# A decode kernel's last weights: the rest of w2 as 128 rows at the end, summed with wo's, and fewer waits on TensorE

## The chip, the cores and the metric

The kernel runs on one core of a Trainium2 chip. The metric is the device time of one execution in microseconds (us), the median of several runs. A profiled execution gives a trace with the instructions of each engine, the DMA packets and the landings of the transfers; a page sums it up. Its span begins with the first instruction and ends with the last one, and the execution's own time is a little longer.

Names used below: TensorE (PE; PEld is its loading of weights), VectorE (DVE), ScalarE (ACT), GpSimd (POOL), and SyncE (SP), which issues most transfers. A landing is the moment at which a transfer's semaphore has its full count of 16, one from each DMA engine.

## What is computed

One decode step of attention with 32 heads over a cache of 4096 keys, beside a dense layer of two matrices with a squared ReLU, mixed by a gate:

```python
g = sigmoid((x * gate_w).sum(-1))
q = x @ wq                                  # 512 -> 32 heads x 128
p = softmax(q . k_cache * 128**-0.5)        # 4096 keys a head
a = (p @ v_cache).reshape(4096) @ wo        # -> 512
r = max(x @ w1 + b1, 0)                     # 512 -> 1376
b = (r * r) @ w2 + b2                       # 1376 -> 512
out = g * a + (1 - g) * b
```

Everything is bfloat16 (both halves take the same x). The key and value caches are 32 MiB each, so nearly all of the kernel's traffic is theirs: 78.3 MB are read from HBM.

## The kernel before

**Tiles.** Four heads form a tile, so there are eight tiles (NT = 8). A tile of keys, and one of values, is 128 partitions by 128 rows of 128 numbers (32 KB a partition, 4 MB in all). A ring of five buffers of that size holds keys and values as they come. SyncE issues the loads in the order of the list LOADS (keys run two tiles ahead of values), each once its buffer is free (`free`, L300 to L308). The last entry but one in the list, "m", is the dense layer's: w1 (1376 KB, L336), the first 1280 rows of w2 with ten rows a partition (1280 KB, L337), and the last 96 rows of w2, one a partition on partitions 0 to 95 (96 KB, L338). After "m" come the values of the last tile, in four parts of 40, 36, 32 and 20 rows a partition (L331, by the table PARTS, L60), and after those the last 512 rows of wo as loads of 384 and 128 KB (L340). The other 3584 rows of wo are brought by GpSimd and SyncE earlier. The output goes out at L343.

**Keys.** The scores are split. VectorE multiplies and sums most rows (L716, 656 of them); the rest is transposed on TensorE (L509), copied out by ScalarE (L415) and multiplied with q (L524). The tile's maximum goes over VectorE and TensorE (`max_rows`, L531; `max_cols`, L536; L730, L733), ScalarE makes the exponentials (L434), and `pv` multiplies them with the values on TensorE (L555): one matmul for each row of the tile, 128 a tile. `den` (L564) sums the denominators, and `norm` (L746) divides and applies the gate.

**The end.** TensorE's order is written out by hand. After the last scores it does, in this order: `turn_a` and `spread_a` (L569, L576: the first 28 heads' results are turned), `out_a` (L585, 88 matmuls of wo into the accumulator `acc`), `max_cols`, `mlp_h` (L600, the first dense layer), `den` for the last tile, `mlp_out` (L612, 44 matmuls: the second dense layer, into its own accumulator `MO`), `pv` for the first part of the last values, `add_v` (L591, rows of wo that VectorE has summed meanwhile at L777 and L781), `pv` for the other three parts, and after `norm` `out_b` (L621, 16 matmuls of wo's rest into `acc`). Each part's `pv` waits for its own landing. VectorE adds `MO` to the scaled bias b2 (L817), later adds `acc` to that (L821), TensorE transposes the sum (L674), and VectorE copies it to where SyncE takes it (L823).

**The dense layer's rest.** 1376 = 10 x 128 + 96. The hidden layer is held as 128 partitions by 11 columns; the eleventh column has 96 rows. `b1c` holds b1 in that form, `mlp_bias` and `mlp` make max(h, 0)*h and multiply it by 1 - g (`omg`, L765).

**Waits.** Each instruction may be preceded by any number of waits on semaphores. In TensorE's part many are covered: by program order, or by another wait, they have always been met when they come. `pm` (L478) makes each use of one PSUM bank wait until the one before has been read.

Of the kernel before, what the change touches and what calls it, by code (L numbers as in the profile page):

```python
# [5 lines left out]
def bass_gated_mix__gqa_block_cached__dense_activation_squared_relu__decode_kernel(  # L6
# [25 lines left out]
    FG = 10  # L32
    FR = F - FG * 128
    SCALE = float(D) ** -0.5


    R = 4
# [21 lines left out]

    PARTS = {NT - 3: [0, 64, B], NT - 2: [0, 32, 64, 96, B], NT - 1: [0, 40, 76, 108, B]}  # L60

# [71 lines left out]
    with ctx:  # L133
# [19 lines left out]
        w2a = held("m")[:, W2:W3].rearrange("p (g n) -> p g n", g=FG)  # L153
        w2b = held("m")[0:FR, W3:W3 + DM]
        W4 = W3 + DM
# [46 lines left out]
        hp = sb("hp", [128, FG + 1], fp32)  # L202
        hs = sb("hs", [128, FG + 1], bf16)
        b2g = sb("b2g", [128, 4], fp32)
        fin = sb("fin", [128, 4], bf16)
# [17 lines left out]
        H = pX[:, 256:256 + FG + 1]  # L223
        MO = pX[:, 288:292]
        B1 = pM[:, 288:288 + FG + 1]
# [54 lines left out]
        s_h = sem("s_h")  # L280
        s_mo = sem("s_mo")
        s_fb = sem("s_fb")
        s_vs = sem("s_vs")
# [27 lines left out]
        def started(eng):  # L311
            eng.wait_ge(s_qps, NT)
            eng.wait_ge(s_g, 4)
            eng.wait_ge(s_b1c, 2)


        @block.sync
        def _(eng):
            for n, (kind, j) in enumerate(LOADS):
                free(eng, n)  # L320
                if n == SLOTS - 1:
                    started(eng)
                    for p, st, k, q in STRIPS[len(RUNS):]:
                        a, b = W[p:p + st * (k - 1) + 1:st, :], woa_v[q:q + k, :]
                        if k == 1:
                            a, b = [v.rearrange("p (a n) -> p a n", a=2) for v in (a, b)]
                        eng.dma_start(a, b).then_inc(s_wr, 16)
                if kind == "v" and j in PARTS:
                    for w in range(len(PARTS[j]) - 1):
                        part = slice(PARTS[j][w] * 128, PARTS[j][w + 1] * 128)  # L330
                        eng.dma_start(held("v", j)[:, part], v_v[j][:, part]).then_inc(s_vl[j, w], 16)  # L331
                elif kind in "kv":
                    eng.dma_start(held(kind, j), (k_v if kind == "k" else v_v)[j])\
                       .then_inc(s_l[n % SLOTS], 16)
                elif kind == "m":
                    eng.dma_start(held("m")[:, 0:W2], w1_v).then_inc(s_w[0], 16)  # L336
                    eng.dma_start(held("m")[:, W2:W3], w2_v).then_inc(s_w[1], 16)  # L337
                    eng.dma_start(w2b, B_w2[FG * 128:F, :]).then_inc(s_w[2], 16)  # L338
            for c in range(len(TS) - 1):
                eng.dma_start(wob_sb[:, TS[c]:TS[c + 1], :], wob_v[:, TS[c]:TS[c + 1], :])\  # L340
                   .then_inc(s_wo[c], 16)
            eng.wait_ge(s_f4, 1)
            eng.dma_start(out[0, 0, :].rearrange("(j p) -> j p", p=128), fin4).then_inc(s_out, 16)  # L343
# [110 lines left out]
        def _(eng):  # L454
# [11 lines left out]
            for n in range(FG + 1):  # L466
                M = 128 if n < FG else FR
                mm = eng.matmul(B1[0:M, n:n + 1], b1r[:, n:FG * 128:FG] if n < FG else b1r[:, FG * 128:F],
                                ident[0:1, 0:1], start=True, stop=True)
# [5 lines left out]

            read = [(s_b1c, 2)]

            def pm(sem, count):  # L478
                for w in read:
                    eng.wait_ge(*w)  # L480
                read[:] = [(sem, count)]
# [15 lines left out]
            def transposes(u):  # L497
# [3 lines left out]
                for k in range(2):  # L501
                    n = 2 * u + k
                    if n >= 3:
                        eng.wait_ge(s_ev, n - 2)
# [8 lines left out]
            def scores(u):  # L513
                j, w = u // U, u % U
                if w == 0:
                    if j >= 2:
                        eng.wait_ge(s_cp, R * (j - 1))
                    eng.wait_ge(s_qc, j + 1)
                for k in range(2):
# [8 lines left out]
            def max_rows(j):  # L528
                eng.wait_ge(s_mp, j + 1)
                pm(s_gm, j + 1)  # L530
                eng.transpose(MT[0:1, :], mp[:, j:j + 1], identf[:, :]).then_inc(s_mt, 1)  # L531

            def max_cols(j):
                eng.wait_ge(s_dg, j + 1)
                pm(s_nm, j + 1)
                eng.matmul(MB[:, j:j + 1], gx[0:1, j % 2, :], onesf[0:1, 0:1],  # L536
# [23 lines left out]
            def den(c):  # L560
                a, b = GR[c]
                eng.wait_ge(s_e, b)
                pm(s_rd, c + 1)
                eng.matmul(DEN[:, a:b], onesf[:, :], RS[:, a:b], start=True, stop=True).then_inc(s_den, 1)  # L564

            def turn_a():
                eng.wait_ge(s_on, NG - 1)
                eng.wait_ge(s_ev, 2 * NU)
                eng.transpose(KP[0][0:NA, 0:128], onorm[:, 0:NA], ident[:, :]).then_inc(s_at, 1)  # L569

            def spread_a():
                eng.wait_ge(s_ac, 1)
                eng.wait_ge(s_cp, R * NT)
                eng.wait_ge(s_sel, 1 + len(STRIPS))
                for c in range(4):
# [4 lines left out]
            def out_a():  # L580
                eng.wait_ge(s_ac, 2)
                eng.wait_ge(s_wk, 1)
                for t in range(TP):
# [10 lines left out]
            def mlp_h():  # L594
                eng.wait_ge(s_w[0], 16)
                for n in range(FG + 1):
                    M = 128 if n < FG else FR
                    for t in range(4):
                        lhs = w1_sb[:, t, n:FG * 128:FG] if n < FG else w1_sb[:, t, FG * 128:F]
                        mm = eng.matmul(H[0:M, n:n + 1], lhs, xcol[:, t:t + 1],  # L600
                                        start=(t == 0), stop=(t == 3))
                mm.then_inc(s_h, 1)

            def mlp_out():
                eng.wait_ge(s_w[1], 16)
                eng.wait_ge(s_w[2], 16)
                eng.wait_ge(s_hs, 1)
                for n in range(FG + 1):
                    M = 128 if n < FG else FR
                    w = w2a[:, n, :] if n < FG else w2b  # L610
                    for j in range(4):
                        mm = eng.matmul(MO[:, j:j + 1], w[:, j * 128:(j + 1) * 128], hs[0:M, n:n + 1],  # L612
                                        start=(n == 0 and j == 0), stop=(n == FG and j == 3),
                                        skip_group_check=True)
                mm.then_inc(s_mo, 1)

            def out_b(c):
                eng.wait_ge(s_wo[c], 16)
                for h in range(TS[c], TS[c + 1]):
                    for j in range(4):  # L620
                        mm = eng.matmul(acc[:, j:j + 1], wob_sb[:, h, j * 128:(j + 1) * 128],  # L621
                                        onorm[:, NA + h:NA + h + 1], start=False, stop=(h == NZ - 1),
                                        skip_group_check=True)
                if c == len(TS) - 2:
                    mm.then_inc(s_acc, 1)

# [37 lines left out]
            den(NG - 1)  # L664
            mlp_out()
            for u in range((NT - 1) * U, NU):
# [4 lines left out]
            for c in range(len(TS) - 1):  # L671
                out_b(c)
            eng.wait_ge(s_fin, 1)
            eng.transpose(KP[2][0:4, 0:128], fin[:, :], ident[:, :]).then_inc(s_fT, 1)  # L674
# [3 lines left out]
        def _(eng):  # L678
            eng.memset(zeros, 0.0).then_inc(s_dz, 1)
            eng.memset(b1c[:, :], 0.0).then_inc(s_dz, 1)  # L680
            eng.wait_ge(s_dz, 2)
            eng.wait_ge(s_x, 32)
            eng.tensor_tensor_reduce(grow, xrow, grow, 1.0, 0.0, ALU.mult,
# [15 lines left out]
            eng.wait_ge(s_b1, 1)  # L699
            eng.tensor_copy(b1c[:, 0:FG], B1[:, 0:FG]).then_inc(s_b1c, 1)  # L700
            eng.tensor_copy(b1c[0:FR, FG:FG + 1], B1[0:FR, FG:FG + 1]).then_inc(s_b1c, 1)

# [49 lines left out]
            def mlp_bias():  # L752
                eng.wait_ge(s_h, 1)
                eng.wait_ge(s_b1c, 2)
                for p, n in cells:
                    eng.tensor_tensor(hr[p, n], H[p, n], b1c[p, n], ALU.add).then_inc(s_hv, 1)

            def mlp():
                eng.wait_ge(s_hv, 1)
                for p, n in cells:  # L760
                    eng.scalar_tensor_tensor(out=hp[p, n], in0=hr[p, n], scalar=0.0, in1=hr[p, n],
                                             op0=ALU.max, op1=ALU.mult).then_inc(s_hv, 1)
                eng.wait_ge(s_hv, 2)
                for p, n in cells:
                    eng.tensor_scalar(hs[p, n], hp[p, n], omg[p, 0:1], None, ALU.mult).then_inc(s_hs, 1)  # L765

# [47 lines left out]
            recip(NG - 1)  # L814
            eng.wait_ge(s_mo, 1)
            eng.wait_ge(s_g, 4)
            eng.tensor_tensor(b2g[:, :], MO, b2g[:, :], ALU.add).then_inc(s_fb, 1)  # L817
            norm(NG - 1)
            eng.wait_ge(s_acc, 1)
            eng.wait_ge(s_fb, 1)  # L820
            eng.tensor_tensor(fin[:, :], acc[:, 0:4], b2g[:, :], ALU.add).then_inc(s_fin, 1)  # L821
# [33 lines left out]
```

## Time and profile before

| | us |
|---|---|
| median of three runs | 193.54 |
| lowest and highest | 193.41, 193.60 |
| the profiled execution | 193.49 |
| its span | 192.1 |

Of the span TensorE is busy for 57% (109.9 us), VectorE for 83%, ScalarE for 43%, GpSimd for 12%. The queue that SyncE feeds moves 75.37 MB in 4452 packets and takes 92.9% of the 16 DMA engines' time; GpSimd's queue moves 2.95 MB, and two queues bring instructions (16 packets with 0.26 MB, and 14 with 0.11 MB). The mean rate is 410 GB/s.

How to read it: in the timeline a line has the start, the time from the first start to the last end, the engine, the line of the kernel, the operation, what it writes and reads, how many there are, and in brackets how long the engine sat idle ahead of it and what ended that. "issue" there means that the engine waited for nothing that the profile shows. In the table by stretches each row has the stretch, its length, the busy time and count of each engine (PE, PEld, DVE, ACT, POOL), the clock granted to TensorE, the busy share of the DMA engines and the GB/s that they moved.

### The profile page before, as it was taken

Reading aid. Unit: us, or ns where it says so; the run is one execution under the profiler, and the core shown is the slowest. Engines: PE = TensorE matmul, PEld = TensorE weight load, DVE = VectorE, ACT = ScalarE, POOL = GpSimd, SP = SyncE. Lnnn points to the kernel's source line nnn. Section 1 sums busy time; section 2 is a strip of 40 time slices with the busy share of each in tenths; the row PEclk is TensorE's granted clock in tenths of the full one; section 3 lists DMA queues with packets and bytes.
Section 4 is the critical chain, followed back from the end, with each engine's and each line's share of the span. In section 5 each row is a group of like instructions: output and inputs, shape, how many; then the busy total and the mean of one; then the engine's idle time right before and its main releaser. Section 6 shows DMA issues by size and latency. Waiting matters only on the chain.

```text
span 192.1 us, 6035 instructions
## 1 busy us (share of the span) xinstructions
PE 109.9 (57%) x2056; PEld 97.1 (51%) x2058; DVE 158.8 (83%) x1387; ACT 82.7 (43%) x204; POOL 22.9 (12%) x56
## 2 busy tenths in 40 slices
PE   0139665544614653397469255935876488449884
PEld 0123344434513542297459145924876378448873
DVE  0310299999999999999999998998999799998721
ACT  2104776743833663078339232933744383001300
POOL 7760000995000000000000000000000000000000
PEclk9999999555555555555555555555855555555555
DMA  6999999999999999999999999999999999999991
GB/s 225 431 437 437 437 438 426 432 438 432 423 428 416 423 432 413 447 404 433 416 432 416 440 428 437 425 421 437 420 421 416 406 426 411 422 418 382 407 386 68
DMA packets 5456, 78.71 MB, mean 410 GB/s; under 512 B 1285, under 2 KB 1895, under 8 KB 2024
## 3 DMA queue, kind: packets, MB, share of 16 engines
q1 hardware_dynamic: 4452, 75.37, 92.9%
q0 software_dynamic: 960, 2.95, 3.8%
q8 instruction: 16, 0.26, 0.6%
q14 instruction: 14, 0.11, 0.1%
q10 hardware_dynamic: 14, 0.01, 0.0%
HBM read 78.32 MB, written 0.00 MB: 408 GB/s over the span
## 4 chain that ended last, share of the span: by engine, by line
DVE 48%; DMA 41%; SPq 6%; PE 3%; issue 1%; DVEq 0%
DVE ring L716 45%; DMA ring<-in_A_k_cache_dram 26%; DMA ring<-in_A_v_cache_dram 15%; SPq L331 5%; DVE S L716 2%; PE pO L555 1%; PE KP L509 1%; DVE gm L730 1%; DVE gx L733 0%; PE pQ L621 0%; PE pM L564 0%; PE pM L536 0%; SPq L337 0%; SPq L338 0%; SPq L294 0%
## 5 line engine op out<-in xcount | busy, mean ns | idle before, releaser
L716 DVE CUSTOM_DVE_ANT_0 ring<-ring,qb 128x128 bf16<-128x128 bf16 x656 | 140.6, 283 | 2.4 <-DMA ring<-in_A_k_cache_dram 2.4
L415 ACT ACTIVATE kT<-KP 128x768 bf16<-128x768 bf16 (+1 forms) x64 | 46.4, 783 | 48.7 <-PE KP L509 48.4
L509 PE MATMUL KP<-ident,ring 128*128 128x128 bf16 x368 | 43.0, 300 | 21.8 <-DMA ring<-in_A_k_cache_dram 18.6
L716 DVE DVE_READ_ACCUMULATOR2_ANT S<- 128x1 f32 x656 | 51.8, 79 | 0.1
L509 PEld LDWEIGHTS KP<-ident,ring 128*128 128x128 bf16 x368 | 35.6, 139 | 23.9 <-DMA ring<-in_A_k_cache_dram 19.0
L555 PE MATMUL pO<-E,ring 128*128 128x4 bf16 x640 | 19.8, 166 | 2.8 <-DMA ring<-in_A_v_cache_dram 2.2
L555 PEld LDWEIGHTS pO<-E,ring 128*128 128x128 bf16 x640 | 18.9, 105 | 3.4 <-DMA ring<-in_A_v_cache_dram 2.4
L434 ACT ACTIVATE E<-S,nM 32x128 bf16<-32x128 f32 x32 | 18.5, 579 | 0.9
L555 PE MATMUL pX<-E,ring 128*128 128x4 bf16 x384 | 11.9, 166 | 4.7 <-DMA ring<-in_A_v_cache_dram 4.7
L555 PEld LDWEIGHTS pX<-E,ring 128*128 128x128 bf16 x384 | 11.3, 103 | 5.2 <-DMA ring<-in_A_v_cache_dram 5.1
L426 ACT ACTIVATE nM<-pM 128x1 f32<-128x1 f32 x8 | 1.4, 170 | 23.0 <-PE pM L536 23.0
L531 PE MATMUL pM<-identf,mp 128*1 128x128 f32 x8 | 3.1, 384 | 13.9 <-DVE mp L723 13.9
L536 PE MATMUL pM<-onesf,gx 1*128 1x1 f32 x16 | 4.5, 345 | 9.1 <-DVE gx L733 9.1
L536 PEld LDWEIGHTS pM<-onesf,gx 1*128 1x128 f32 x16 | 3.8, 291 | 9.8 <-DVE gx L733 9.7
L524 PE MATMUL pQ<-qcol,kT 128*128 128x4 bf16 x176 | 7.8, 170 | 1.0 <-ACT kT L415 0.9
L531 PEld LDWEIGHTS pM<-identf,mp 128*1 128x1 f32 x8 | 0.7, 91 | 15.2 <-DVE mp L723 15.0
L524 PEld LDWEIGHTS pQ<-qcol,kT 128*128 128x128 bf16 x176 | 7.6, 111 | 1.3 <-ACT kT L415 1.3
L434 ACT ACTIVATION_READ_ACCUMULATOR E<-S,nM 32x1 f32 x32 | 8.1, 253 | 0.0
L386 POOL MEMSET tick<- 1x1 f32 x1 | 0.1, 90 | 66.9 <-DMA W<-in_A_wo_dram 66.9
L378 POOL DMA_DIRECT2D W<-in_A_wo_dram x14 | 8.0, 574 | 0.0
L524 PE MATMUL pS<-qcol,kT 128*128 128x4 bf16 x192 | 7.8, 168 | 0.0
L363 POOL TENSOR_SCALAR_AFFINE_SELECT selA<-selA 28x36 bf16<-28x36 bf16 (+6 forms) x22 | 7.4, 335 | 3.2 <-POOL selA L358 0.2
(83 smaller groups left out, 97.6 us busy)
## 6 DMA issues: line engine op xcount, KB each, us to landing
ring<-in_A_k_cache_dram SPq DMA_DIRECT2D x8, 4096.0 KB, 30.1
ring<-in_A_v_cache_dram SPq DMA_DIRECT2D x5, 4096.0 KB, 29.2
ring<-in_A_v_cache_dram SPq DMA_DIRECT2D x5, 1024.0 KB, 28.8
W<-in_A_wq_dram SPq DMA_DIRECT2D x1, 4096.0 KB, 12.6
ring<-in_A_v_cache_dram SPq DMA_DIRECT2D x2, 2048.0 KB, 27.5
W<-in_A_wo_dram POOLq DMA_DIRECT2D x2, 768.0 KB, 18.2
ring<-in_B_w_dram SPq DMA_DIRECT2D x1, 1376.0 KB, 25.0
ring<-in_B_w_dram SPq DMA_DIRECT2D x1, 1280.0 KB, 28.2
```

The source lines that it names most:

```text
L331: eng.dma_start(held("v", j)[:, part], v_v[j][:, part]).then_inc(s_vl[j, w], 16)
L363: eng.affine_select(out=part, in_=part, compare_op=ALU.not_equal, fill=1.0, base=-st * q, pattern=[[st, 4], [-1, st * (k - 1) + 1]], chann ...
L378: eng.dma_start(W[p:p + st * (k - 1) + 1:st, :], woa_v[q:q + k, :], max_dma_last_dim=16384).then_inc(s_wp[n], 16)
L415: eng.activation(kT[:, n % NC, 0:HB[u // U] * 128], KP[n % 3][:, 0:HB[u // U] * 128], ACT.Copy).then_inc(s_ev, 1)
L434: eng.activation(E[rows, j % NE, :, r], S[rows, j % NS, :], ACT.Exp, bias=nM[rows, j:j + 1], scale=SCALE, accum_out=RS[rows, R * j + r:R * ...
L509: mm = eng.transpose(KP[n % 3][:, y * 128:(y + 1) * 128], held("k", j)[:, b * 128:(b + 1) * 128], ident[:, :])
L524: mm = eng.matmul(S2[j % 2][:, c:c + R], kT[:, n % NC, y * 128:(y + 1) * 128], qcol[:, R * j:R * j + R], start=True, stop=True)
L531: eng.transpose(MT[0:1, :], mp[:, j:j + 1], identf[:, :]).then_inc(s_mt, 1)
L536: eng.matmul(MB[:, j:j + 1], gx[0:1, j % 2, :], onesf[0:1, 0:1], start=True, stop=True).then_inc(s_mb, 1)
L555: mm = eng.matmul(O(R * j, R * j + R), held("v", j)[:, b * 128:(b + 1) * 128], E[:, j % NE, b, :], start=(b == 0), stop=(b == B - 1), skip ...
L716: ins = eng.tensor_tensor_reduce(kb, kb, qb[:, j, :], 1.0, 0.0, ALU.mult, ALU.add, S[:, j % NS, b:b + 1])
L730: eng.tensor_reduce(g, MT[0:1, :].rearrange("a (r p) -> a r p", r=R), AX.X, ALU.max)\
```

## The change

- The load of w2's rest takes the last 128 rows of w2 (rows 1248 to 1375) instead of the last 96, on all 128 partitions, and is issued after wo's rest instead of ahead of the last values: 128 KB for 96 KB.
- The 32 rows that are thereby loaded twice count once: the hidden layer's eleventh column now has 128 rows too (the last 128 columns of w1, the last 128 numbers of b1), and a new tile `omw`, 1 - g everywhere and 0 in the first 32 rows of that column, replaces `omg` in the product (L765).
- The second dense layer is summed into `acc`, where wo's sums are, so `MO`, the semaphores s_mo and s_fb and VectorE's addition (L817) go. Its first ten columns (40 matmuls) stay where they were; the four matmuls of the eleventh come after `out_b`, and carry the semaphore that lets VectorE make `fin`.
- The last tile's values come in parts of 40, 40, 36 and 12 rows.
- On TensorE 31 covered waits are dropped: in `transposes`, `scores`, `max_rows`, `max_cols`, `den`, `turn_a`, and `spread_a` (which takes over the wait for wo's rows from `out_a`).

```diff
-    PARTS = {NT - 3: [0, 64, B], NT - 2: [0, 32, 64, 96, B], NT - 1: [0, 40, 76, 108, B]}
+    PARTS = {NT - 3: [0, 64, B], NT - 2: [0, 32, 64, 96, B], NT - 1: [0, 40, 80, 116, B]}
...
-        w2b = held("m")[0:FR, W3:W3 + DM]
+        w2b = held("m")[:, W3:W3 + DM]
...
-                    eng.dma_start(w2b, B_w2[FG * 128:F, :]).then_inc(s_w[2], 16)
             for c in range(len(TS) - 1):
                 eng.dma_start(wob_sb[:, TS[c]:TS[c + 1], :], wob_v[:, TS[c]:TS[c + 1], :])\
                    .then_inc(s_wo[c], 16)
+            eng.dma_start(w2b, B_w2[F - 128:F, :]).then_inc(s_w[2], 16)
...
-            def pm(sem, count):
+            def pm(sem, count, covered=()):
                 for w in read:
-                    eng.wait_ge(*w)
+                    if w[0] not in covered:
+                        eng.wait_ge(*w)
...
-                    if n >= 3:
+                    if k and n >= 3:
                         eng.wait_ge(s_ev, n - 2)
...
-                if w == 0:
-                    if j >= 2:
-                        eng.wait_ge(s_cp, R * (j - 1))
-                    eng.wait_ge(s_qc, j + 1)
+                if u == 0:
+                    eng.wait_ge(s_qc, 1)
...
-                pm(s_gm, j + 1)
+                pm(s_gm, j + 1, (s_qc, s_nm, s_rd))
...
-                pm(s_nm, j + 1)
+                pm(s_nm, j + 1, (s_gm,))
...
-                pm(s_rd, c + 1)
+                pm(s_rd, c + 1, (s_nm,) if c >= NG - 2 else ())
...
-                eng.wait_ge(s_ev, 2 * NU)
...
-                eng.wait_ge(s_cp, R * NT)
-                eng.wait_ge(s_sel, 1 + len(STRIPS))
+                eng.wait_ge(s_wk, 1)
...
-                        lhs = w1_sb[:, t, n:FG * 128:FG] if n < FG else w1_sb[:, t, FG * 128:F]
-                        mm = eng.matmul(H[0:M, n:n + 1], lhs, xcol[:, t:t + 1],
+                        lhs = w1_sb[:, t, n:FG * 128:FG] if n < FG else w1_sb[:, t, F - 128:F]
+                        mm = eng.matmul(H[:, n:n + 1], lhs, xcol[:, t:t + 1],
...
+            def mlp_out(n):
+                if n in (0, FG):
+                    eng.wait_ge(s_w[1 if n < FG else 2], 16)
+                if n == 0:
+                    eng.wait_ge(s_hs, 1)
+                w = w2a[:, n, :] if n < FG else w2b
+                for j in range(4):
+                    mm = eng.matmul(acc[:, j:j + 1], w[:, j * 128:(j + 1) * 128], hs[:, n:n + 1],
+                                    start=False, stop=(n == FG), skip_group_check=True)
+                if n == FG:
+                    mm.then_inc(s_acc, 1)
...
             den(NG - 1)
-            mlp_out()
+            for n in range(FG):
+                mlp_out(n)
...
             for c in range(len(TS) - 1):
                 out_b(c)
+            mlp_out(FG)
...
+            eng.memset(omw[:, :], 1.0).then_inc(s_dz, 1)
...
+            eng.memset(omw[0:FO, FG:FG + 1], 0.0).then_inc(s_dz, 1)
...
+            eng.tensor_copy(b1c[:, :], B1).then_inc(s_b1c, 1)
+            eng.wait_ge(s_dz, 3)
+            eng.tensor_scalar(omw[:, :], omw[:, :], omg[:, 0:1], None, ALU.mult).then_inc(s_g, 1)
...
-                    eng.tensor_scalar(hs[p, n], hp[p, n], omg[p, 0:1], None, ALU.mult).then_inc(s_hs, 1)
+                    eng.tensor_tensor(hs[p, n], hp[p, n], omw[p, n], ALU.mult).then_inc(s_hs, 1)
...
-            eng.wait_ge(s_mo, 1)
-            eng.wait_ge(s_g, 4)
-            eng.tensor_tensor(b2g[:, :], MO, b2g[:, :], ALU.add).then_inc(s_fb, 1)
             norm(NG - 1)
             eng.wait_ge(s_acc, 1)
-            eng.wait_ge(s_fb, 1)
+            eng.wait_ge(s_g, 4)
             eng.tensor_tensor(fin[:, :], acc[:, 0:4], b2g[:, :], ALU.add).then_inc(s_fin, 1)
```

## The prediction

> **What bounds the kernel now.** I read the 40 slices of the page first: from 5 us to 187 us the 16 DMA engines are busy, so the transfers set the pace, whatever the chain of waits says (it runs through VectorE because VectorE frees the buffers, but the queue always holds work).
>
> ```profile
> DMA  6999999999999999999999999999999999999991
> GB/s 225 431 437 437 437 438 426 432 438 432 423 428 416 423 432 413 447 404 433 416 432 416 440 428 437 425 421 437 420 421 416 406 426 411 422 418 382 407 386 68
> DVE 48%; DMA 41%; SPq 6%; PE 3%; issue 1%; DVEq 0%
> ```
>
> The rate is not even: slice 37 (173 to 178 us) falls to 382. The table by stretches shows where (last three columns: TensorE clock, DMA share, GB/s).
>
> ```profile
> 173.00:174.00 1.00, 0.71 (x9) 0.31 (x9) 0.55 (x4) 0.00 (x0) 0.00 (x0) 0.50 1.01 425
> 174.00:175.00 1.00, 1.00 (x40) 1.00 (x41) 0.93 (x4) 0.00 (x0) 0.00 (x0) 0.50 1.04 389
> 175.00:176.00 1.00, 1.00 (x44) 1.00 (x41) 0.96 (x2) 0.00 (x0) 0.00 (x0) 0.50 1.04 346
> 176.00:177.00 1.00, 1.00 (x20) 0.97 (x18) 0.96 (x2) 0.03 (x1) 0.00 (x0) 0.50 1.01 374
> 177.00:178.00 1.00, 1.00 (x20) 1.00 (x19) 0.93 (x3) 0.94 (x4) 0.00 (x0) 0.50 1.04 368
> 178.00:179.00 1.00, 1.00 (x21) 1.00 (x19) 0.75 (x1) 0.97 (x4) 0.00 (x0) 0.50 0.97 389
> 179.00:180.00 1.00, 0.68 (x11) 0.59 (x9) 0.25 (x2) 0.60 (x4) 0.00 (x0) 0.50 0.99 418
> ```
>
> The engines are full, but move less: against 420 the five stretches lack 31+74+46+52+31 = 234 KB, or 0.56 us. The trace's packet records say what runs there. The 1 KB packets of the 96-row load of w2 (L338) go through eight of the engines from 174.30 to 175.65 and through the other eight from 176.26 to 177.97; the 10,240-byte packets beside them, on all engines, take 450 to 550 ns instead of 385, from 174.8 to 176.1 and from 176.8 to 178.3: the same two intervals, 0.4 to 0.5 us later, about the time from a packet's end to its landing (wo's last packet ended at 189.31 and landed at 189.73). Other 1 KB packets do no such harm: the two loads of wo's rest (L340, 128 partitions) raise the 5,120-byte packets beside them from 196 to at most 205 ns. Nor is it the arithmetic: out_a and mlp_h (L585, L600) run on past the ends of the two intervals, and VectorE's L781 runs again from 180.27 at 412 to 436 GB/s.
>
> The end of the kernel, by the timeline:
>
> ```profile
> 186.66 1.25 PE L555 MATMUL pO<-E,ring 128*128 128x4 bf16 x35 [0.48 <-issue]
> ...
> 188.45 0.69 PE L555 MATMUL pO<-E,ring 128*128 128x4 bf16 x20 [0.54 <-DMA ring<-in_A_v_cache_dram]
> 189.25 0.22 DVE L746 SCALAR_TENSOR_TENSOR onorm<-pO,gcol,rden 128x4 bf16<-128x4 f32 x1 [5.73 <-PE pO L555]
> ...
> 189.54 0.57 PE L621 MATMUL pQ<-onorm,ring 128*128 128x1 bf16 x16 [0.40 <-DVE onorm L746]
> 190.15 0.16 DVE L821 TENSOR_TENSOR fin<-pQ,b2g 128x4 bf16<-128x4 f32 x1 [0.68 <-PE pQ L621]
> ```
>
> The last values land at 188.40; 20 matmuls, norm, 16 matmuls of wo, fin. Two clocks run here side by side: landing records of the slowest engine give w1 174.61, w2 178.21, its 96 rows 178.52, the four value parts 181.57, 184.35, 186.85, 188.40, wo's rest 189.41 and 189.73. The 13th wo matmul needs the last of these and starts at about 189.86 (189.54 plus 12 steps of 0.027), only 0.13 us later.
>
> **The change, part by part** (against the profiled run: span 192.1, time 193.49, so 1.39 lies around it; the median shown is 193.54, 0.05 above).
>
> *The load of w2's rest.* It leaves its place before the last values: -0.31 on everything behind (178.52 - 178.21). It comes back as 8 rows an engine at the end: wo's last 128 KB are the same shape, 189.73 - 189.41 = +0.32. What becomes of the slowing is not shown, so both ends: it goes wholly, or follows the load to the end. The slowest engine took 178.21 - 174.61 = 3.60 us for w2's 1280 KB and 181.57 - 178.52 = 3.05 for the first value part, also 1280 KB: 0.55 is the price, as the table gave. I take -0.54, because the nearest row for 1 KB packets on 128 partitions at the end (wo's rest) shows no slowing. Last landing: 189.73 - 0.31 - 0.54 + 0.32 = 189.20.
>
> The Trainium skill gives a reason: "DMA: Bandwidth & Descriptors", The descriptor swizzle, has each DMA engine of a 128-partition transfer write one SBUF port of its own, and its section on why a DMA increments its semaphore by 16 spreads 96 partitions over 16 engines too, six each, which then can't match the ports' eights. By that rule the slowing belongs to the 96 rows and the first rival below would have no chance; the trace agrees in time and place, but all engines slow alike, where a clash of ports would pick some, so that rival keeps the chance that the rows give it.
>
> SP: the four value parts are issued one issue (0.47 us) earlier, and w2's load after L340's second, which ends at 174.65. Even if that issue takes 7.6 us as its neighbour's did, it is out by 182.3, seven us ahead of its landing. SP's next task, the output, comes at 190.9.
>
> *Parts 40, 40, 36, 12.* No bytes change. Moved by -0.85 and the sizes (9,216 to 10,240 bytes a row: +0.27; 8,192 to 9,216: +0.28; both by the landings of the old parts; 5,120 to 3,072: -0.55, which closes the sum), the parts land at 180.72, 183.77, 186.55 and 187.55. Part 1 waits for mlp_out anyway (181.8), part 2 for add_v (185.16, which waits for VectorE's L781, untouched). Part 3 starts at 186.60, 36 steps of 0.027 end at 187.6; the last 12 start then, the last of them at 187.9. From there before's own distances: 0.28 to norm, 0.29 to wo: 188.47; the first wo load lands at 189.41 - 0.85 = 188.56, so 188.6. 16 matmuls: the last at 189.03, after the landing of wo's second load at 188.88. The 20-matmul step lost eight, 0.21 us, but this chain is no longer the later one.
>
> *Second layer summed into wo's accumulator.* Its last four matmuls move behind wo's and wait for the last landing, 189.20: start 189.25, the fourth at 189.35. Behind that wait on TensorE stand only the final transpose, and fin on VectorE. Before, the last wo matmul started at 189.95. So **-0.60**. VectorE loses L817 (0.13 us at 183.38, in a wait of 5.73: worth nothing). Without cover by the landing, the four extra matmuls would cost 0.11.
>
> *Start.* VectorE gets a memset and a 0.15 us multiply (as L694) and one copy of b1c instead of two (0.17 + 0.14): it waits from 14.0 to 17.4 for qcol. hs by a product of tensors: 0.17 (as L756) for 0.23, while TensorE waits; 0. The last column group of w1 and b1 as 128 columns: same count of matmuls; 0.
>
> *31 waits.* TensorE is idle 43% of the span and is ended by data; 0 directly. But they move something: code. The instruction queue fetched 16 blocks of 16 KB. In before, TensorE stops inside part 2 of the values, where nothing waits: 33 matmuls, 0.65 us, then three more at 186.66 (the "issue" line). The stop before that is den at 180.22, 0.5 after its input; between them lie 127 matmuls and 127 weight loads and a few waits, one block. The packet records have fetches at 177.61 and 184.30, each about 1.06 long. So a block comes 6.4 us after the block before it was entered. Today it hides: part 3 lands at 186.85. With 31 slots fewer (if each wait is one) and 8 moved behind, the stop moves 39 slots, to after the 13th matmul of part 3, which runs at 186.97. The block before is entered between 180.2, as now, and 180.6 (its own predecessor's start moves 15 matmuls, 0.4, back in out_a), so the code is there at 186.6 to 187.0. From that matmul to the last one of all it is 2.0 us (23 + 12 + 20 steps, norm and its gaps), and the last one waits for data until 189.35: code up to 187.3 costs nothing. I take 0.
>
> The Trainium skill's "Runtime: NRT & Kernel Launch", Instruction fetch mechanics, gives TensorE room for 2048 instructions and calls the fetch hidden; by it this cost would be nil at any place. By it the last two rivals below would have no chance; the trace disagrees (0.65 us in the middle of 36 matmuls).
>
> **Sum:** 193.49 - 0.60 = 192.89 for the profiled run; 192.94 by the median. Forecast 192.95.
>
> **The rivals.**
> - *The slowing follows the load,* or its cause is another and it stays. For: it came with these bytes of w2, and 128 rows are a third more. Against: wo's rest. Then the last landing is 189.73 - 0.31 + 0.32 = 189.74, up to +0.18 with a third more: 193.45 to 193.75, 0.22.
> - *TensorE takes over.* Code after 187.3, so that the last matmul starts 2.0 after it; at 187.6 that is 189.6: -0.35, 193.2. For: the stop above. Against: the slack. 193.1 to 193.4, 0.14; a slowing that goes only in part ends here too.
> - *Slower: the code comes much later.* Place: after the 13th matmul of part 3; price: each us late, one us, from 187.3 on; it decides at 187.95 (no gain left), and costs 0.4 at 188.35. For: after it no landing covers a stop. Against: that asks for 7.8 us from block to block where the trace has 6.4. 193.95 and above, 0.07.
>
> **How the numbers follow.** Forecast 0.57 (192.75 to 193.1). Range: from 0.2 below the forecast (slice rates alone vary by that) up to 193.6, most of the first rival; left out are the third, the rest of the first and a little below. 0.2% is 0.39 us, about what a measurement of this kernel can tell from no change. Faster by more means below 193.15: the forecast and a third of the second rival, 0.62. Within: 0.30. Slower: 0.08.
>
> **What would show it.** Right: 410 or more GB/s through w1, w2 and the first value part; part 1 landed near 180.7; the last four L612-like matmuls starting some 0.3 us after wo's, released by the load. Wrong: packets of 450 ns or more beside the 1 KB ones at the end (first rival), or an "issue" gap within the 36 matmuls of part 3 (the others). If the rate at 174 to 178 stays low with the load gone, its cause was another, and the time stays near 193.5.

## The result

| | before | after |
|---|---|---|
| median of six runs each, us | 193.56 (193.39 to 193.66) | 192.91 (192.84 to 193.23) |
| the profiled execution, us | 193.49 | 192.9 |
| its span, us | 192.1 | 191.5 |

The ratio after/before is 0.9973, with a 95% interval from 0.9962 to 0.9985: faster by about 0.5 us (0.3 to 0.7). The forecast was 192.95, within 192.75 to 193.6.

The page of the changed kernel, the same three lines as were shown of before (DMA share and GB/s in 40 slices, then the chain by engine):

```profile
DMA  6999999999999999999999999999999999999992
GB/s 226 432 438 438 438 440 428 438 411 450 411 443 411 421 412 421 438 429 431 414 447 421 428 426 428 431 417 424 428 419 424 411 428 409 421 415 428 417 382 70
DVE 48%; DMA 40%; SPq 7%; PE 3%; issue 1%; DVEq 0%
```

Slice 37 has gone from 382 to 428 GB/s. The others are what they were, to within the wobble of single slices (up to some 30 either way). In the stretches (columns as before, the last is GB/s):

```profile
174.00:175.00 1.00, 1.00 (x42) 1.00 (x41) 0.93 (x4) 0.00 (x0) 0.00 (x0) 0.50 1.05 440
175.00:176.00 1.00, 1.00 (x44) 1.00 (x41) 0.96 (x2) 0.00 (x0) 0.00 (x0) 0.50 1.05 440
176.00:177.00 1.00, 1.00 (x20) 0.97 (x18) 0.96 (x2) 0.06 (x1) 0.00 (x0) 0.50 0.95 399
177.00:178.00 1.00, 1.00 (x20) 1.00 (x20) 0.93 (x3) 0.94 (x4) 0.00 (x0) 0.50 1.11 457
178.00:179.00 1.00, 1.00 (x20) 1.00 (x20) 0.73 (x1) 0.95 (x4) 0.00 (x0) 0.50 0.90 369
```

Single rows swing (457 beside 369), because a packet's bytes are booked in one stretch. So the mean of the five is what counts: 421 GB/s, where before had 373. TensorE, VectorE and ScalarE do the same there as before, so the arithmetic is not what made the difference.

The end of the kernel, by the timeline:

```profile
186.71 1.44 PE L553 MATMUL pO<-E,ring 128*128 128x4 bf16 x48 [0.66 <-DMA ring<-in_A_v_cache_dram]
188.26 0.22 DVE L741 SCALAR_TENSOR_TENSOR onorm<-pO,gcol,rden 128x4 bf16<-128x4 f32 x1 [5.10 <-PE pO L553]
...
188.70 0.57 PE L614 MATMUL pQ<-onorm,ring 128*128 128x1 bf16 x16 [0.55 <-DMA ring<-in_A_wo_dram]
...
189.26 0.27 PE L605 MATMUL pQ<-hs,ring 128*128 128x1 bf16 x4
189.57 0.16 DVE L814 TENSOR_TENSOR fin<-pQ,b2g 128x4 bf16<-128x4 f32 x1 [1.09 <-PE pQ L605]
```

Parts 3 and 4 of the values are now one row of 48 matmuls with no gap, neither an "issue" stop nor a wait for part 4. The wo matmuls wait for their own load. The last of them starts at 189.10, and the last four, of w2's rest, wait for theirs, which lands at 189.22. The addition `fin` starts at 189.57, where it started at 190.15: 0.58 us earlier, which is the difference of the spans (0.6).

The landings of the slowest engine (us), measured in these profiled executions, with the two experiments that come to lie nearest to the change:

| | before | predicted | after | form alone | 128 rows, old place |
|---|---|---|---|---|---|
| first 1280 rows of w2 | 178.21 | | 177.66 | 177.56 | 177.79 |
| w2's rest | 178.52 | 189.20 | 189.22 | 177.86 | 178.14 |
| part 1 of the last values | 181.57 | 180.72 | 180.74 | 180.94 | 181.22 |
| part 2 | 184.35 | 183.77 | 183.82 | 183.72 | 184.29 |
| part 3 | 186.85 | 186.55 | 186.67 | 186.23 | 187.11 |
| part 4 | 188.40 | 187.55 | 187.59 | 187.78 | 188.06 |
| wo's rest, first load | 189.41 | 188.56 | 188.56 | 188.77 | 189.00 |
| wo's rest, second load | 189.73 | 188.88 | 188.89 | 189.09 | 189.30 |

### The profile page after: what moved, and what is told of

It reads as the page before. It is cut to its first block, busy times and chain, and to the rows that moved or that the text cites. A ratio compares the mean times of both kernels' runs of the same rounds, so it can differ in the third digit from the quotient of the medians.

```text
span 191.5 us, 6005 instructions
## 1 busy us (share of the span) xinstructions
PE 111.0 (58%) x2058; PEld 97.6 (51%) x2058; DVE 159.0 (83%) x1387; ACT 82.7 (43%) x204; POOL 22.7 (12%) x56
## 4 chain that ended last, share of the span: by engine, by line
DVE 48%; DMA 40%; SPq 7%; PE 3%; issue 1%; DVEq 0%
DVE ring L711 45%; DMA ring<-in_A_k_cache_dram 26%; DMA ring<-in_A_wo_dram 14%; SPq L331 6%; DVE S L711 2%; PE pO L553 1%; PE KP L509 1%; DVE gm L725 1%; DVE gx L728 0%; PE pM L562 0%; PE pM L534 0%; PE pQ L614 0%; SPq L337 0%; SPq L294 0%; DVE mp L718 0%
## 5 line engine op out<-in xcount | busy, mean ns | idle before, releaser
L711 DVE DVE_READ_ACCUMULATOR2_ANT S<- 128x1 f32 x656 | 49.7, 76 | 0.1
L522 PEld LDWEIGHTS pS<-qcol,kT 128*128 128x128 bf16 x192 | 7.8, 108 | 0.2
```

Of the source, the lines that this page charges most:

```text
L522: mm = eng.matmul(S2[j % 2][:, c:c + R], kT[:, n % NC, y * 128:(y + 1) * 128], qcol[:, R * j:R * j + R], start=True, stop=True)
L711: ins = eng.tensor_tensor_reduce(kb, kb, qb[:, j, :], 1.0, 0.0, ALU.mult, ALU.add, S[:, j % NS, b:b + 1])
```

## The experiments

The theory behind the prediction, called A in the expectations: the 96-row load, which covers 96 of the 128 partitions, slows every packet beside it while it runs, and 128 rows do not. The rivals: the slowing belongs to the place in the stream, or to the bytes (B), or the gain came from something else that the change touched (C: waits, parts, the common sum). Each kernel below was run beside the kernel before; the ratio is to that, with its 95% interval.

A measure that is used throughout, called the packet measure, is worked out from the trace's packet records. It is each packet's time above the fast tenth of the packets of its size, summed over the packets that start from 174 to 180 us, divided by the 16 engines. It gives 0.64 us for before and 0.07 us for after. The difference, 0.56, is the price of the load beyond its own bytes, and the same as the prediction's 0.56 from the GB/s.

### The form alone

Before, with the last 128 rows on 128 partitions at the old place; `omw` and the 128-column forms come with it. Accumulator, parts and waits stay.

```diff
-        w2b = held("m")[0:FR, W3:W3 + DM]
+        w2b = held("m")[:, W3:W3 + DM]
...
-                    eng.dma_start(w2b, B_w2[FG * 128:F, :]).then_inc(s_w[2], 16)
+                    eng.dma_start(w2b, B_w2[F - 128:F, :]).then_inc(s_w[2], 16)
...
```

> The kernel before with one part of the change: w2's rest is loaded as 128 rows on 128 partitions, at its old place ahead of the last values; second layer, parts and waits as before. Theory A (the 96-partition form slows all packets): the stretch 174 to 178 us moves 410 GB/s or more, w2's rest lands within 0.5 us of w2, the first value part lands near 181.1 (181.57 - 0.54 + 0.09), wo's rest at 188.95 and 189.27; the end is then 20 matmuls, norm and wo's 16: the last wo matmul starts near 189.5 instead of 189.95, ratio 0.9977. Theory B (any small load of these bytes at this place slows the rest): the stretch stays near 370, everything 0.09 later, ratio 1.0005. Theory C (the gain came from parts, waits or the common sum): ratio 1.000.

Measured: 0.9982 (0.9973 to 0.9990). The load moves a third more bytes at the same place, and two of the stretches that lacked most read:

```profile
175.00:176.00 1.00, 1.00 (x43) 1.00 (x41) 0.96 (x2) 0.00 (x0) 0.00 (x0) 0.50 1.08 442
177.00:178.00 1.00, 1.00 (x20) 1.00 (x20) 0.93 (x3) 0.94 (x4) 0.00 (x0) 0.50 1.05 427
```

Before had 346 and 368 there. The five stretches from 174 to 179 us average 411 GB/s (before: 373), and the packet measure is 0.10 us. So the form is enough to take nearly all of the slowing away. The end of this kernel, by its timeline:

```profile
186.24 1.09 PE L556 MATMUL pO<-E,ring 128*128 128x4 bf16 x35 [0.48 <-issue]
187.83 0.70 PE L556 MATMUL pO<-E,ring 128*128 128x4 bf16 x20 [0.50 <-DMA ring<-in_A_v_cache_dram]
188.91 0.59 PE L621 MATMUL pQ<-onorm,ring 128*128 128x1 bf16 x16 [0.39 <-DVE onorm L748]
189.54 0.16 DVE L824 TENSOR_TENSOR fin<-pQ,b2g 128x4 bf16<-128x4 f32 x1 [0.68 <-PE pQ L621]
```

Here the chain from the last values sets the end, as in before, only 0.63 us earlier (wo's matmuls at 188.91 instead of 189.54). Its profiled span is 191.5, the same as that of the whole change, and its `fin` comes as early (189.54, where after has 189.57).

### All but the form

After, with the 96-row form: the load stays at the end and covers partitions 0 to 95 again; the common sum, the parts and the dropped waits stay.

```diff
-        w2b = held("m")[:, W3:W3 + DM]
+        w2b = held("m")[0:FR, W3:W3 + DM]
...
-            eng.dma_start(w2b, B_w2[F - 128:F, :]).then_inc(s_w[2], 16)
+            eng.dma_start(w2b, B_w2[FG * 128:F, :]).then_inc(s_w[2], 16)
...
```

> The changed kernel with one part undone: w2's rest is again 96 rows on 96 partitions, but at its new place at the end. Theory A: the slowing comes back at the end; packets of wo's rest beside it take 50 to 80 ns instead of 46, and the last landing, which 32 KB less would bring to 189.13, comes at 189.3 to 189.7; ratio to before 0.998 to 1.000. Theory B (place, not form): no slowing, last landing 189.13, ratio 0.9965, a little below the changed kernel's 0.9973.

Measured: 0.9978 (0.9969 to 0.9987), between what the two theories gave. At 174 to 179 us nothing is slow (410, 430, 440, 406, 430 GB/s). At the end the packets that start from 186 to 188 us are slowed by 0.10 us an engine where after has 0.02. So the load does carry its harm along, but at a seventh of the price, 0.08 for 0.56. Few other packets are left for it to slow: the queues move 281 and 224 GB/s from 186 to 188 us, at a DMA share of 0.85 and 0.65. The last landing is at 189.22, as in after, although 32 KB less are moved. The other thing that this timeline shows:

```profile
185.43 1.80 PE L554 MATMUL pO<-E,ring 128*128 128x4 bf16 x52
187.49 1.10 PE L554 MATMUL pO<-E,ring 128*128 128x4 bf16 x36 [0.27 <-issue]
188.98 0.58 PE L617 MATMUL pQ<-onorm,ring 128*128 128x1 bf16 x16 [0.39 <-DVE onorm L745]
189.43 0.24 PE L608 MATMUL pQ<-hs,ring 96*128 96x1 bf16 x4
```

After 12 of part 3's 36 matmuls TensorE stops and goes on at 187.49. The block of instructions that it lacks began to be fetched at 184.91, where after has 184.13. From there on the chain runs without a wait for data: wo's matmuls are released by norm, and `fin` comes at 189.71, 0.14 behind after, though the last landing is the same. So in this execution the stop, and not the load, made the difference. This is the prediction's second rival, in a sister of the changed kernel.

### The waits alone, the parts alone

Before with the covered waits dropped, as in the change, and nothing else; and before with the new table of parts and nothing else.

```diff
-    PARTS = {NT - 3: [0, 64, B], NT - 2: [0, 32, 64, 96, B], NT - 1: [0, 40, 76, 108, B]}
+    PARTS = {NT - 3: [0, 64, B], NT - 2: [0, 32, 64, 96, B], NT - 1: [0, 40, 80, 116, B]}
```

> The kernel before with the 31 covered waits dropped and nothing else. Theories A and B: transfers unchanged, ratio 1.000 (within 0.0006); TensorE's stop after 33 of the 36 matmuls of part 2 goes, as the code boundary moves 31 slots into part 3, where the code is there in time. Theory C: ratio 0.998 or less.

> The kernel before with the last values in parts of 40, 40, 36 and 12 rows and nothing else. Theories A and B: no byte less, the last part lands at 188.4 as before, eight matmuls fewer stand behind it (-0.21), but wo's last load at 189.73 then holds the last four matmuls: the last starts at 189.86 instead of 189.95, ratio 0.9996. Theory C: the whole -0.2 or more, ratio 0.999 or less.

Measured: waits 0.9997 (0.9988 to 1.0006), parts 1.0005 (0.9996 to 1.0014): neither moves the time. Both keep the slowing (315 to 429 and 323 to 413 GB/s at 174 to 179 us). With the waits dropped, part 2's 36 matmuls run through; TensorE waits for part 3 instead:

```profile
185.27 1.10 PE L554 MATMUL pO<-E,ring 128*128 128x4 bf16 x36
186.98 1.01 PE L554 MATMUL pO<-E,ring 128*128 128x4 bf16 x32 [0.61 <-DMA ring<-in_A_v_cache_dram]
```

With the parts changed, the last values land earlier (188.26), but the bytes behind them are the same, and TensorE now waits for wo's load:

```profile
186.91 1.91 PE L555 MATMUL pO<-E,ring 128*128 128x4 bf16 x55 [0.75 <-issue]
189.41 0.57 PE L621 MATMUL pQ<-onorm,ring 128*128 128x1 bf16 x16 [0.59 <-DMA ring<-in_A_wo_dram]
```

### All but the place

After, with its 128-row load put back ahead of the last values.

```diff
                     eng.dma_start(held("m")[:, W2:W3], w2_v).then_inc(s_w[1], 16)
+                    eng.dma_start(w2b, B_w2[F - 128:F, :]).then_inc(s_w[2], 16)
...
-            eng.dma_start(w2b, B_w2[F - 128:F, :]).then_inc(s_w[2], 16)
```

> The changed kernel with one part undone: the 128-row load is issued at its old place, ahead of the last values; form, sum, parts and waits as changed. Theory A: no slowing at either place; the same bytes, so the last landing is the same 189.2 but is now wo's; four wo matmuls and w2's last four stand behind it instead of four: the last matmul starts 0.11 later than in the changed kernel, and the values land 0.33 later: ratio to before 0.9978 to 0.9980. Theory B (place): the slowing of 0.54 is back at 174 to 178, ratio 1.000.

Measured: 0.9983 (0.9975 to 0.9992). No slowing at the old place (417, 418, 408, 441, 389 GB/s). Everything behind the load lands 0.41 to 0.48 us later than in after: 0.35 is its own time (between the landings of w2's first rows and of its rest), and w2's first rows were 0.13 later already. Wo's first load sets the end:

```profile
189.13 0.56 PE L614 MATMUL pQ<-onorm,ring 128*128 128x1 bf16 x16 [0.53 <-DMA ring<-in_A_wo_dram]
189.56 0.24 PE L605 MATMUL pQ<-hs,ring 128*128 128x1 bf16 x4
189.84 0.16 DVE L814 TENSOR_TENSOR fin<-pQ,b2g 128x4 bf16<-128x4 f32 x1 [0.91 <-PE pQ L605]
```

`fin` is at 189.84, 0.27 later than in after, of which 0.13 was there ahead of the load. The rest, 0.14, is what the place is worth once the form is right, by one profiled execution each; the intervals of the ratios (0.9983 and 0.9973) overlap. Against the form alone (0.9982), the common sum, the parts and the dropped waits give nothing at the old place.

### What about the load slows the others

Five variants of before's load, each at its place. They bring other bytes, or bring w2's elsewhere, so the second layer's last column is no longer w2's and the output is another; only transfers and times are compared. Each stands in the stead of

```diff
-                    eng.dma_start(w2b, B_w2[FG * 128:F, :]).then_inc(s_w[2], 16)
```

First the same 96 KB as 768 bytes on each of 128 partitions:

```diff
+                    flat = B_w2[FG * 128:F, :].rearrange("r n -> (r n)").rearrange("(p m) -> p m", p=128)
+                    eng.dma_start(held("m")[:, W3:W3 + 384], flat).then_inc(s_w[2], 16)
```

Then 96 rows of another matrix, wo, in the old form:

```diff
+                    eng.dma_start(w2b, A_wo[0:FR, :]).then_inc(s_w[2], 16)
```

Then 64 partitions by 1536 bytes (and likewise 32 by 3072), to columns that nothing reads:

```diff
+                    flat = B_w2[FG * 128:F, :].rearrange("r n -> (r n)").rearrange("(p m) -> p m", p=64)
+                    eng.dma_start(held("m")[0:64, W5 + 256:W5 + 256 + 768], flat).then_inc(s_w[2], 16)
```

Last, 96 rows on partitions 32 to 127, to those columns:

```diff
+                    eng.dma_start(held("m")[32:128, W5 + 256:W5 + 256 + DM], B_w2[FG * 128:F, :]).then_inc(s_w[2], 16)
```

> The kernel before, in which the same 96 KB of w2 are read at the same place but written as 768 bytes on each of 128 partitions instead of 1024 on each of 96; the last column of the second layer so multiplies other numbers than w2's rest, and part of what it reads is not loaded. Theory A (rows on 96 partitions, six an engine): no slowing, w2 lands near 177.7 and the first value part near 181.0; ratio 0.997 to 0.998. If the bytes of w2 that are read are what slows (a place in HBM): unchanged, the stretch near 370 GB/s, ratio 1.000.

> The kernel before, in which the load at this place brings 96 rows of wo in place of w2's rest, in the same form on the same partitions; the second layer multiplies these instead of w2's rest. Theory A: the slowing is the same (stretch near 370 GB/s, 10,240-byte packets of 450 to 550 ns), ratio 1.000. If the source in HBM is the cause: no slowing, ratio 0.9975.

> The kernel before, in which the same 96 KB of w2 are written as 1536 bytes on each of 64 partitions (four an engine) to an unused place; the second layer's last column so reads what lay there before. Theory P (engines write among the partitions of others): still slow, as engines 8 to 15 would write to partitions 32 to 63; the stretch 174 to 178 near 370 GB/s, ratio 0.999 to 1.001. Theory O (six rows an engine, not a power of two, is the trouble): no slowing, first value part near 181.0, ratio 0.997 to 0.998.

> As the one with 64 partitions, with 3072 bytes on each of 32 partitions (two an engine). Theory P: slow, at least as much, since all 96 KB now go to a quarter of the partitions: ratio 1.000 to 1.002. Theory O: no slowing, ratio 0.997 to 0.998.

> The kernel before with the 96-row load written to partitions 32 to 127 instead of 0 to 95, at an unused place; the second layer's last column reads what lay there before. Theories P and O alike: slow as before, ratio 1.000. If partitions 0 to 31 as such are the trouble: no slowing, ratio 0.9975.

| the load, 96 KB each | ratio to before | GB/s in the five stretches from 174 to 179 | packet measure, us |
|---|---|---|---|
| before: 96 partitions (0 to 95) x 1024 B | 1 | 389, 346, 374, 368, 389 | 0.64 |
| 128 x 768 B | 0.9970 (0.9958 to 0.9981) | 433, 409, 415, 423, 403 | 0.11 |
| 96 x 1024 B, rows of wo | 0.9998 (0.9989 to 1.0007) | 424, 342, 356, 375, 371 | 0.63 |
| 64 x 1536 B | 1.0008 (0.9999 to 1.0017) | 386, 318, 331, 354, 405 | 0.74 |
| 32 x 3072 B | 1.0015 (1.0004 to 1.0026) | 397, 335, 326, 345, 407 | 0.77 |
| 96 x 1024 B, partitions 32 to 127 | 1.0000 (0.9989 to 1.0010) | 385, 350, 376, 335, 411 | 0.63 |

The stretch from 175 to 176 us, first of the load on 128 partitions, then of the one on 64:

```profile
175.00:176.00 1.00, 1.00 (x44) 1.00 (x42) 0.96 (x2) 0.00 (x0) 0.00 (x0) 0.50 1.00 409
```

```profile
175.00:176.00 1.00, 1.00 (x44) 1.00 (x42) 0.93 (x3) 0.00 (x0) 0.00 (x0) 0.50 1.03 318
```

The engines are as full (last column but one, 1.00 and 1.03), and the instructions are the same; only the bytes differ. The very same bytes of w2, in smaller packets but on all partitions, slow next to nothing (0.11 us, where the kernel without the load has 0.08). So it is not where they lie in HBM; nor is it the size of the packets, as 1024 B on 128 partitions (the form alone) do no harm either. Another matrix's rows in the old form do the same harm as w2's. Two readings of the form stood against each other. By O, the trouble is that 96 rows make a share of six for each engine, which is no power of two; shares of four (64 partitions) and two (32) ought then to do less. They do a little more (by the packet measure 0.74 and 0.77 us where before has 0.64), so O falls. By P, any load that leaves partitions out does it; it holds in all five. And which 96 partitions they are, 0 to 95 or 32 to 127, makes no difference.

### Twice, and not at all

Before with the 96-row load issued a second time, to columns that nothing reads; and before without the load and without the wait for it, so that the second layer's last column reads what lay there before.

```diff
                     eng.dma_start(w2b, B_w2[FG * 128:F, :]).then_inc(s_w[2], 16)
+                    eng.dma_start(held("m")[0:FR, W5 + 256:W5 + 256 + DM], B_w2[FG * 128:F, :]).then_inc(s_w[2], 16)
...
-                eng.wait_ge(s_w[2], 16)
+                eng.wait_ge(s_w[2], 32)
```

```diff
-                    eng.dma_start(w2b, B_w2[FG * 128:F, :]).then_inc(s_w[2], 16)
...
-                eng.wait_ge(s_w[2], 16)
```

> The kernel before with the 96-row load issued twice in a row, the second copy to an unused place of the same partitions. Theory A, if the price goes with the packets: another 0.26 us of packets and another 0.5 of slowing, so the values land 0.8 later, ratio 1.004. If only the step from one transfer to the next costs, or the load is harmless: 0.26 later, ratio 1.0013.

> The kernel before without the load of w2's rest and without the wait for it; the second layer's last column reads what lay there before. The load's whole price: its packets (0.31) and the slowing (0.54) if nothing else follows: the values land 0.85 earlier (first part near 180.7), wo's rest at 188.88; the last wo matmul near 189.2 instead of 189.95; ratio 0.996. If the slowing comes from another thing in this stretch: 0.31 earlier, ratio 0.9984.

Measured: twice 1.0041 (1.0025 to 1.0056), not at all 0.9960 (0.9947 to 0.9973). One load more costs as much as one load less gains, 0.8 us by either, where 96 KB at 420 GB/s make 0.23. The stretches of the kernel with two loads show it beside before's 346 and 389:

```profile
175.00:176.00 1.00, 1.00 (x43) 1.00 (x41) 0.96 (x2) 0.00 (x0) 0.00 (x0) 0.50 1.11 308
...
178.00:179.00 1.00, 1.00 (x21) 1.00 (x20) 0.56 (x1) 0.94 (x5) 0.00 (x0) 0.50 0.90 321
```

By the packet measure the second load adds 0.37 us, less than the first's 0.56; with its bytes that is 0.6, and the rest of the 0.8 lies within the interval. In the profiled execution, the fastest of the four with two loads, wo's last load landed 0.34 later than in before.

## Why the prediction was right

- **What bounds the kernel.** Shown. Without the load the stretches from 174 to 179 us move 379 to 440 GB/s, with one 346 to 389, with two 308 to 380. The price that the prediction read from the stretches (0.56) and from the slowest engine (0.54) is the 0.56 that the packets lost. Two of its readings of packets are off, and the term doesn't hang on them. By their starts the slow 10,240-byte packets of before lie from 174.4 to 176.1 and from 176.4 to 178.1 us and take 400 to 555 ns, so they set in 0.1 to 0.2 us behind the first 1 KB packet, not 0.4 to 0.5. And of the 5,120-byte packets beside wo's rest two take 345 and 538 ns, all others 206 or less.
- **The load of w2's rest** (-0.31, -0.54, +0.32). The predicted last landing was 189.20, and it was 189.22. The choice of the end at which the slowing goes wholly, made from the wo loads beside it, was right: the excess at the end is 0.02 us an engine.
- **That the place would matter for the slowing** was not needed. The prediction put the two edits of the load into one term, but either one takes most of the slowing away. By the packet measure the 0.64 us of before become 0.10 with the form alone, 0.08 with all but the form and 0.07 with both; the ratios are 0.9982, 0.9978 and 0.9973. They are two cures of one ill and do not add up. What the place gives beyond the form is not shown. Four matmuls instead of twenty then stand behind the bytes that set the end, and the expectation put that at 0.11 us. Counted from the landing of w2's first rows, `fin` comes after 11.91 us in the changed kernel, 11.98 with the form alone and 12.05 with all but the place: about that much, but by one profiled execution each, and the intervals of the ratios overlap.
- **Parts.** The four landings came within 0.12 us of what was worked out; the largest miss is part 3 (186.67 for 186.55). Alone the parts gave nothing, as said. They matter only beside the new place, where the chain from the last values has to stay ahead of wo's load: norm ended at 188.48 and wo's matmuls began at 188.70, released by the load. The prediction had 188.6; it allowed 0.05 from landing to matmul where this wait took 0.14. The miss cost nothing, since the last four matmuls waited for a later landing.
- **The sum in `acc`, VectorE's addition, the start.** The last four matmuls began at 189.26 (189.25 predicted), released by their load. No kernel had the common sum alone; with the parts and the dropped waits, at the old place, it gave nothing (0.9983, and 0.9982 without them).
- **The waits and the code.** Alone they gave nothing. The traces show that 61 waits go on TensorE (265 become 204), not 31; the 31 are those that were instructions of their own (62 become 31), while the others rode on another instruction. For the length of the code the 31 are what counts, so the prediction's 39 slots stand: with 96 rows at the end the stop came after 52 matmuls of parts 2 and 3, where 33 and half of 39 make 52.5. The side effect was seen: the stop moved from part 2 to where something waits. From the start of a block's fetch to TensorE's going on it is 2.36 us in before (184.30 to 186.66), 2.37 with the form alone, 2.60 with the parts alone, 2.58 with 96 rows at the end. In after the fetch starts at 184.13, so the code is there at 186.5 to 186.7; TensorE is past the place that the prediction gave for the boundary, 13 matmuls of 0.03 into part 3, at 187.1, and does not stop there nor elsewhere in the last values. By that the margin is 0.4 to 0.6 us. With 96 rows at the end, where the stop came after 12 matmuls, the fetch began 0.78 later than in after, and used it up. The prediction measured another way, 6.4 us from the start of `den`. In the ten kernels that stop at before's place this is 6.3 to 7.0, and 7.0 from its own 180.2 to 180.6 would be 187.2 to 187.6, about the 187.3 at which the code begins to cost. So the term was less safe than the 6.4 made it look, and that it came out at nothing is in part luck.
- **The first rival** (the slowing follows the load, 193.45 to 193.75) was half right. The harm does go with the form, but 128 rows have none to carry, and for 96 rows the rival's price was that of mid-stream: at the end it is 0.08 us by the packet measure, instead of 0.56.
- **The reason that the prediction cited.** In the Trainium skill, "DMA: Bandwidth & Descriptors", The descriptor swizzle, each engine of a 128-partition transfer writes one SBUF port of its own. The runs agree so far as it goes: at the old place, loads on 128 partitions leave the packet measure at 0.10 to 0.11 us, and loads on 96, 64 and 32 bring it to 0.63 to 0.77. But no run looked at a port. A clash at ports is an inference; what is shown is that leaving out partitions is the condition, for loads of 96 KB at this place. Whether the number of partitions does it, or which engine writes to which of them, was not told apart.

**Open.** By what way a load on fewer partitions slows the packets of all 16 engines (in before every 10,240-byte packet that starts from 174.6 to 175.6 us takes 459 ns or more, where 385 is the usual), and why 32 partitions cost hardly more than 64, is not settled. Nor is the gain of the place beyond the form, about 0.1 us by single profiles.

## What to carry to other kernels

Look at GB/s in narrow stretches while the DMA engines are full: a stretch that moves less at the same share points to a transfer that slows the others. Give also the small loads in a full stream all 128 partitions, even if that means loading a few rows twice (128 KB instead of 96 KB made this kernel faster by 0.2%), or put them where little else is left to slow. When an edit adds or drops instructions, waits too, ask where the stops for code move to, and whether something waits there anyway.

## What the runs showed of the hardware

- A load of 96 KB, 0.12% of the kernel's bytes, cost 0.4% of its time on 96 partitions in a full stream (no load: 0.9960). On all 128 (128 x 768 B: 0.9970) it cost about 0.2 us, near the 0.23 of its own bytes; the intervals of the two ratios overlap, so this price is rough.
- From the first packet of a block of TensorE's code to its going on it took 2.36 to 2.60 us beside the other transfers, in the kernels that stopped for it. The stop costs nothing where data are late anyway, and shows up when they come sooner. In the kernel without the load, part 3 landed at 186.24, and the matmuls went on 0.6 us later:

```profile
186.84 1.67 PE L554 MATMUL pO<-E,ring 128*128 128x4 bf16 x55 [0.48 <-issue]
```

- In that profiled execution the stop, not a landing, set the end: wo's matmuls began at 188.89, released by norm, though the first of wo's loads had landed at 188.70.
